# Attention scores in three half-height products per half of the keys, with the keys loaded once

## Chip, core and metric

The kernel runs on one core of a Trainium2 chip. The metric is the device time of one execution in microseconds (us); the median of three runs of the kernel before is 776.71 us (776.66 to 779.36). The core's engines are TensorE (PE in the profile, with its weight loads as a row of their own, PEld), VectorE (DVE), ScalarE (ACT), GpSimd (POOL), and SyncE (SP), which here only issues DMAs.

## What is computed

Attention over 16 heads (2 batches of 8, 576 keys, 64 values per head) in which each query keeps its 32 largest scores, then two dense stages on the result: an expert stage with four experts, and a stage that takes the largest of three products.

```python
scores = scale * np.matmul(q, k.transpose(0, 1, 3, 2))        # (2, 8, 576, 576), 64 summed
kth = np.partition(scores, -32, axis=-1)[..., -32:-31]
scores = np.where(scores >= kth, scores, -1e9)
attn = softmax(scores)                                         # with 1e-9 in the divisor
x = (attn @ v), heads side by side                             # (1152, 512)
for e in range(4):
    out += p[:, e:e+1] * (np.maximum(x @ w1[e], 0) @ w2[e])    # w1 512x1024, w2 1024x512
h = np.maximum(np.maximum(out @ m1, out @ m2), out @ m3)       # m 512x768
y = h @ mo                                                     # 768x512
```

All of it is float32. The kernel keeps float32's accuracy on TensorE by splitting every factor into a rounded high part and a low part (the rest), both of the type fp32r, and by summing products of the parts.

## The kernel before

**Attention** goes by pairs: a pair is one tile of 128 query rows and one head pair `hp` (two heads, `j` = 0 and 1; `hp` runs over 4). There are 9 tiles and so 36 pairs. Tile 4 holds rows of both batches, and its scores are made for each batch and summed (`SLOTS` pads with zeros), so its products are twice as many. Time is divided into slots, eight for a pair; `attention()` puts each step of a pair at a slot: scores 4 to 12 slots ahead of the pair's own first slot, then top-32 on DVE (`topk`, four MAX8 and three MATCH_REPLACE8 per head, L389 and L391), the exponential on ACT, the mask on DVE or POOL (L409, L412, L413), the transposes of the probabilities on PE (`trans_p`, L427 and L432), their copies on ACT (`pt`, L430 and L435), the product with the values (`pv`, L469 and L472) and the transpose of the divisors (`trans_r`, L455).

**Scores** (`Pair.scores`, L368): the queries `qT` = (`qh`, `ql`) lie twice, on rows 0 to 63 and again on rows 64 to 127. The keys lie as `kT`, high part on rows 0 to 63 and low part on rows 64 to 127. So one product over 128 rows gives `ql`·(high + low), a second gives `qh`·(high + low). A head's 576 scores are two halves of 288 columns, each in a PSUM bank of its own (`bank`, six of them): two products for each half, four for a head and batch. All four use the whole array of 128 rows by 128 columns.

**Keys** (`load_k`, `split_k`): `twice` loads the same 64 rows of a head pair to both halves of the partitions (2 DMAs, 14 of them with 288 KB and 4 with 144 KB at the start); ACT rounds all 128 rows (L270, one instruction of 576 columns a head), and POOL subtracts on rows 64 to 127 (L271, one of 64x576 a head). There are 8 such key tiles; the first is split by DVE.

**`pv`** is worth a look, since it is the one place that already divides the array: L472 has the two heads' values, 64 columns each, as weights of products that write rows 0 to 63 and rows 64 to 127 of one bank. They are float32 proper, and each stands in the trace as two products. L469 ahead of them and L455 behind them use the whole array.

**The dense stages** run as a generator, `products()`, in seven phases (four expert phases, three of the last stage); each of their products is three of fp32r (L606 to L608). The planner keeps two clocks: `dve(n)` adds the VectorE time of what was issued, `pe(n)` adds n / 2400 us for n columns on TensorE. After each slot the dense stage is advanced until `clock["pe"]` has caught up with `clock["dve"]`. So the order on PE depends on what `pe()` was told that the scores cost, and it is fixed when the program is built: each engine takes its instructions in that order. ACT, POOL and DVE split the weights (L229, L235); the last stage's weights come as 64-bit numbers and are narrowed in 48 pieces (L200 to L212) during and after the last pairs.

Of the kernel before, what the change touches and what calls it, by code (L numbers as in the profile page):

```python
# [10 lines left out]
F32 = mybir.dt.float32  # L11
F32R = mybir.dt.float32r
U32 = mybir.dt.uint32
I32 = mybir.dt.int32
AF = mybir.ActivationFunctionType
ALU = mybir.AluOpType
# [35 lines left out]
def kernel(  # L52
# [14 lines left out]
    nc = tc.nc  # L67
    B, HP, D, _, S = k.shape
    NT, DM = out.shape
    E = gates.shape[2]  # L70
    P = 128
    KT = DM // P
    FF, FF2 = w1.shape[1] * 256, mo.shape[0] * 256
    SH = S // 2
# [16 lines left out]
    kv = ctx.enter_context(tc.tile_pool(name="kv", bufs=2))  # L91
# [22 lines left out]
    def pe(n):  # L114
        clock["pe"] += n / 2400.0

    def bank(name):
        return pg.tile([P, 512], F32, tag="g", name=name)
# [128 lines left out]
    kraw, kT, vt, qraw, qT = {}, {}, {}, {}, {}  # L247
# [5 lines left out]
    def twice(out, src):  # L253

        for half in range(2):
            nc.sync.dma_start(out=out[half * D:(half + 1) * D], in_=src)

    def load_k(b, hp, heads=slice(0, 2)):
        if not heads.start:
            kraw[b, hp] = kv.tile([P, 2, S], F32, tag="kraw", bufs=1, name="kraw")  # L260
        twice(kraw[b, hp][:, heads], k[b, hp][:, heads])

    def split_k(b, hp, heads=(0, 1), sub=nc.gpsimd.tensor_tensor):

        t = kraw[b, hp]
        if 0 in heads:
            kT[b, hp] = kv.tile([P, 2, S], F32R, tag="kT", bufs=5, name="kT")
        d = kT[b, hp]
        for j in heads:
            nc.scalar.activation(out=d[:, j], in_=t[:, j], func=AF.Copy)  # L270
            sub(out=d[D:, j], in0=t[D:, j], in1=d[D:, j].bitcast(F32), op=ALU.subtract)  # L271

    def load_v(b, hp):
        t = kv.tile([P, 2 * NR, D], F32, tag="v", bufs=5, name="vt")
# [39 lines left out]
    def load_first():  # L314
        for j in range(2):
            load_k(0, 0, slice(j, j + 1))
            load_q(0, 0, slice(j, j + 1))

    def split_first():
        for j in range(2):  # L320
            split_k(0, 0, (j,), nc.vector.tensor_tensor)
            split_q(0, 0, slice(j, j + 1), nc.vector.tensor_tensor)
# [26 lines left out]
    class Pair:  # L349
# [10 lines left out]
        def scores(self, j):  # L360
            srcs = [(b, i) for i, (t, b) in enumerate(SLOTS[self.c]) if t == self.t]
            qs = qT[self.c, self.hp]
            halves = []
            for h in range(2):
                ps = bank("pss")
                mm = [(qs[a][:, j, i * P:(i + 1) * P], kT[b, self.hp][:, j, h * SH:(h + 1) * SH]) for b, i in srcs for a in (1, 0)]
                for i, (l, r) in enumerate(mm):
                    nc.tensor.matmul(ps[:, 0:SH], lhsT=l, rhs=r, start=i == 0, stop=i == len(mm) - 1)  # L368
                pe(SH * len(mm))
                halves.append(ps)  # L370
            s = at.tile([P, 2, SH], F32, tag="s%d" % j, bufs=AHEAD_S, name="s")
            self.s[j] = s

            def copy():
                for h in range(2):
                    nc.scalar.activation(out=s[:, h, :], in_=halves[h][:, 0:SH], func=AF.Copy)
                self.did.add(("s", j))
            return copy
# [115 lines left out]
    def attention():  # L494
# [18 lines left out]
        for key, n in first_use.items():  # L513
            s0 = 8 * n
            if n == 0:
                if key[0] == "k":
                    at_slot(-60, load_first)
                    at_slot(-50, split_first)
                    free["k"] = free["q"] = -50
                    at_slot(s0, load_v, *key[1:])  # L520
                continue
            load, split = (load_k, split_k) if key[0] == "k" else (load_q, split_q)
            at = max(s0 + options(n)["scores"] - (SPLIT_K if key[0] == "k" else SPLIT_Q), free[key[0]] + 2)
            at_slot(max(at - LOAD, free[key[0]] + 1), load, *key[1:])
            at_slot(at, split, *key[1:])
            free[key[0]] = at
            if key[0] == "k":
                at_slot(s0, load_v, *key[1:])
# [110 lines left out]
    def hidden(N):  # L639
        if 2 * N <= 512:  # L640
            ht = hp_.tile([P, 2, 512], F32R, tag="h", bufs=4, name="h")
            return ht[:, 0, 0:2 * N], ht[:, 1, 0:2 * N]

        assert len(x_ready) == len(CHUNKS) * HP and 2 * N <= 2 * MAXS * P
        turn[0] += 1
        hh = kv.tile([P, 2, S], F32R, tag="kT", bufs=5, name="hh")
        hl = qp.tile([P, 2, MAXS * P], F32R, tag=("qh", "ql")[turn[0] % 2], name="hl")
        return [x.rearrange("p a n -> p (a n)")[:, 0:2 * N] for x in (hh, hl)]

    def layer2(ps, wts, hs, N, ti, first=True, last=True):  # L650

# [6 lines left out]
    def experts(n, c):  # L658
# [9 lines left out]
        def half1(i, u):  # L668
            for groups in layer1(weight((c, "a", i, u)), (xh[c], xl[c]), begin.pop((i, u), None)):
                if groups is None:  # L670
                    tick()
                    yield True
            hh, hl = hidden(N)
            count = made_h[0] = made_h[0] + 1
            if ON_POOL_H and not count % ON_POOL_H:
                raw = ms.tile([P, 2 * MAXT * P], F32, tag="tm", bufs=2, name="raw")
                later(lambda: [nc.scalar.activation(out=raw[:, g], in_=ps, func=AF.Relu) for g, ps in groups],
                      lambda: [nc.scalar.activation(out=hh[:, 0:2 * N], in_=raw[:, 0:2 * N], func=AF.Copy),
                               nc.gpsimd.tensor_tensor(out=hl[:, 0:2 * N], in0=raw[:, 0:2 * N], in1=hh[:, 0:2 * N].bitcast(F32), op=ALU.subtract),
                               made.add(("h", n, i, u))])  # L680
                yield hh, hl
                return
            dve(2 * N)
            later(lambda: [nc.scalar.activation(out=hh[:, g], in_=ps, func=AF.Relu) for g, ps in groups],
                  *[lambda: None] * H_LAG,
                  lambda: [nc.vector.scalar_tensor_tensor(out=hl[:, g], in0=ps, scalar=0.0, in1=hh[:, g].bitcast(F32),
                                                          op0=ALU.max, op1=ALU.subtract) for g, ps in groups]
                  + [made.add(("h", n, i, u))])
            yield hh, hl
# [92 lines left out]
    def largest(n, c):  # L782
# [6 lines left out]
        for j in range(FF2 // 256):  # L789

            sub = (nc.vector if j == FF2 // 256 - 1 or (2, c) == PHASES[-1] else nc.gpsimd).tensor_tensor
            hh, hl = hidden(N)
            tm = ms.tile([P, 2 * MAXT * P], F32, tag="tm", bufs=2, name="tm")
            for i in range(3):
                yield from converted(j, i)
                for groups in layer1(weight((c, "c", j, i)), x2):
                    if groups is None:
                        tick()
                    yield True
                dve(2 * N if i else 0)  # L800

                def evac(i=i, groups=groups, tm=tm):
                    for g, ps in groups:
                        if i == 0:
                            nc.scalar.activation(out=tm[:, g], in_=ps, func=AF.Copy)
                        else:
                            nc.vector.tensor_tensor(out=tm[:, g], in0=ps, in1=tm[:, g], op=ALU.max)
                todo = [evac]
                if i == 2:
                    todo += [lambda tm=tm, hh=hh: nc.scalar.activation(out=hh, in_=tm[:, 0:2 * N], func=AF.Copy),  # L810
                             lambda tm=tm, hh=hh, hl=hl, sub=sub: sub(out=hl, in0=tm[:, 0:2 * N], in1=hh.bitcast(F32), op=ALU.subtract)]
                later(*todo)
            hs.append((hh, hl))
# [119 lines left out]
```

## Time and profile before

| what | value |
|---|---|
| median of 3 runs | 776.71 us |
| the profiled execution, its own time | 778.73 us |
| its span, first to last instruction | 776.9 us |
| PE busy / PEld busy | 725.2 us (93%) / 655.3 us (84%) |
| DVE busy | 659.9 us (85%) |
| POOL busy | 541.4 us (70%) |
| ACT busy | 482.3 us (62%) |
| mean granted TensorE clock | 0.978 of full speed |

Busy shares over the whole span say little here, since the program has three stretches. Up to about 94 us only attention runs; from there to about 470 us attention and the expert stage run side by side; behind that the dense stages are alone. Matmuls overlap in the trace: a product's own duration is longer than the distance to the next one's start, and what a product costs in a row of products is that distance, start to start.

### The profile page before, as it was taken

The numbers are of one execution on the slowest core, as the hardware profiler recorded it, in microseconds if no ns is written. First come the engines' busy times: TensorE is split into PE (matmuls) and PEld (weight loads), VectorE is DVE, ScalarE is ACT, GpSimd is POOL, SyncE is SP. The second block draws the span as 40 slices with busy tenths as digits, with TensorE's granted clock in tenths as the row PEclk, the third lists the DMA queues.
The fourth block names the chain that finished last, engine by engine and source line by source line (L and its number), as shares of the span: only waits on it lengthen the run. The fifth ranks groups of instructions, "written<-read, shape, count | busy, mean of one in ns | idle before, by whom it ended". The sixth has DMA issues, their size and how long they took to land. (4 is left out here: it accounts for less than half of the span.)

```text
span 776.9 us, 13519 instructions
## 1 busy us (share of the span) xinstructions
PE 725.2 (93%) x4646; PEld 655.3 (84%) x4646; DVE 659.9 (85%) x1247; ACT 482.3 (62%) x1021; POOL 541.4 (70%) x440
## 2 busy tenths in 40 slices
PE   3666799999999999998999998999999999999998
PEld 2545689988998988887998997989998799899996
DVE  6999999999999999999999996898899994243341
ACT  5666768767786876766777675655565643342441
POOL 3887988889998878778878695675677673343430
PEclk9986699999999999999999999999999999999999
DMA  4430255466645446263554454977667864362421
GB/s 117 105 111 1 60 147 162 137 179 163 195 142 177 126 148 180 87 180 107 150 145 137 137 163 153 301 233 250 221 215 260 252 204 136 102 211 92 156 91 40
DMA packets 48612, 119.91 MB, mean 154 GB/s; under 512 B 7840, under 2 KB 18080, under 8 KB 48544
## 3 DMA queue, kind: packets, MB, share of 16 engines
q1 hardware_dynamic: 40336, 110.40, 46.6%
q10 hardware_dynamic: 8208, 8.65, 3.2%
q8 instruction: 36, 0.59, 0.3%
q14 instruction: 32, 0.26, 0.1%
HBM read 110.38 MB, written 8.65 MB: 153 GB/s over the span
## 5 line engine op out<-in xcount | busy, mean ns | idle before, releaser
L235 POOL TENSOR_TENSOR wlo<-raw,whi 128x512 fp32r<-128x512 f32 x260 | 359.7, 1413 | 129.8 <-ACT whi L229 128.9
L229 ACT ACTIVATE whi<-raw 128x1024 fp32r<-128x1024 f32 x164 | 170.3, 1057 | 41.1 <-DMA raw<-in_w_dram 16.7
L389 DVE MAX8 m<-work 128x8 f32<-128x576 f32 x216 | 154.1, 739 | 0.1
L606 PE MATMUL ps<-xl,whi 128*128 128x256 f32 (+1 forms) x512 | 153.6, 300 | 0.0
L608 PE MATMUL ps<-xh,wlo 128*128 128x256 f32 (+1 forms) x512 | 151.3, 296 | 0.0
L607 PE MATMUL ps<-xh,whi 128*128 128x256 f32 (+1 forms) x512 | 151.2, 295 | 0.0
L235 DVE TENSOR_TENSOR wlo<-raw,whi 128x1024 fp32r<-128x1024 f32 x34 | 52.7, 1550 | 67.2 <-ACT whi L229 55.9
L391 DVE MATCH_REPLACE8 work<-m,work 128x576 f32<-128x576 f32 x144 | 106.0, 736 | 0.0
L607 PEld LDWEIGHTS ps<-xh,whi 128*128 128x128 f32 x512 | 97.2, 190 | 0.9
L606 PEld LDWEIGHTS ps<-xl,whi 128*128 128x128 f32 x512 | 97.1, 190 | 1.0
L608 PEld LDWEIGHTS ps<-xh,wlo 128*128 128x128 f32 x512 | 97.1, 190 | 0.0
L606 PE MATMUL ps<-wlo,h 128*128 128x512 f32 x192 | 77.6, 404 | 0.0
L608 PE MATMUL ps<-whi,h 128*128 128x512 f32 x192 | 75.4, 392 | 0.0
L607 PE MATMUL ps<-whi,h 128*128 128x512 f32 x192 | 75.3, 392 | 0.0
L409 DVE SCALAR_TENSOR_TENSOR p<-s,m,p 128x576 f32<-128x576 f32 x57 | 73.8, 1295 | 0.0
L608 PE MATMUL ps<-x2h,wlo 128*128 128x384 f32 x216 | 72.8, 337 | 0.0
L606 PE MATMUL ps<-x2l,whi 128*128 128x384 f32 x216 | 72.7, 337 | 0.0
L607 PE MATMUL ps<-x2h,whi 128*128 128x384 f32 x216 | 72.6, 336 | 0.0
L368 PE MATMUL pss<-kT,ql 128*128 128x288 f32 x160 | 54.7, 356 | 14.1 <-DVE ql L312 7.5
L212 POOL TENSOR_TENSOR narrow<-narrow,raw 128x256 int32<-128x256 int32 x48 | 40.3, 840 | 39.3 <-DVE narrow L209 10.5
L427 PE MATMUL psp<-ident,p 128*128 128x128 f32 x288 | 49.1, 298 | 17.8 <-POOL p L413 11.9
L427 PEld LDWEIGHTS psp<-ident,p 128*128 128x128 f32 x288 | 37.3, 153 | 24.4 <-POOL p L413 15.5
(97 smaller groups left out, 1632.6 us busy)
## 6 DMA issues: line engine op xcount, KB each, us to landing
raw<-in_w_dram SPq DMA_DIRECT2D x128, 512.0 KB, 3.7
raw<-narrow SPq DMA_DIRECT2D x36, 512.0 KB, 3.4
raw<-in_m_dram SPq DMA_DIRECT2D x36, 256.0 KB, 4.9
narrow<-narrow ACTq DMA_DIRECT2D x48, 128.0 KB, 4.4
kraw<-in_k_dram SPq DMA_DIRECT2D x14, 288.0 KB, 4.5
raw<-in_mo_dram SPq DMA_DIRECT2D x12, 256.0 KB, 4.3
out_dram<-ob ACTq DMA_DIRECT2D x9, 256.0 KB, 2.0
vt<-in_v_dram SPq DMA_DIRECT2D x8, 256.0 KB, 3.7
```

The costliest lines, as they stand in the source:

```text
L212: nc.gpsimd.tensor_tensor(out=out.bitcast(I32), in0=out.bitcast(I32), in1=last, op=ALU.add)
L229: nc.scalar.activation(out=hi, in_=raw, func=AF.Copy)
L235: on.tensor_tensor(out=lo[:, x], in0=raw[:, x], in1=hi[:, x].bitcast(F32), op=ALU.subtract)
L368: nc.tensor.matmul(ps[:, 0:SH], lhsT=l, rhs=r, start=i == 0, stop=i == len(mm) - 1)
L389: nc.vector.max(m[:, 8 * r:8 * r + 8], src)
L391: nc.vector.match_replace(out=self.w[j], in_to_replace=m[:, 8 * r:8 * r + 8], in_values=src, imm_value=NEG)
L409: nc.vector.scalar_tensor_tensor(out=p, in0=s, scalar=kth, in1=p, op0=ALU.is_ge, op1=ALU.mult, accum_out=total)
L427: nc.tensor.transpose(ps[:, r * P:(r + 1) * P], self.p[:, part, part * TAIL + r * P:part * TAIL + (r + 1) * P], ident)
L606: nc.tensor.matmul(ps, lhsT=lh, rhs=rl, start=first, stop=False)
L607: nc.tensor.matmul(ps, lhsT=lh, rhs=rh, start=False, stop=False)
L608: nc.tensor.matmul(ps, lhsT=ll, rhs=rh, start=False, stop=last)
```

## The change

The low part of the keys no longer lies beside the high part on other rows. The new `kT` has four fields for each row: head, part (high, low), and 288 columns. Rows 0 to 63 hold the first half of the keys (columns 0 to 287), rows 64 to 127 the second half. For a head and batch there are now three terms for each half, `ql`·high, `qh`·low and `qh`·high, each a product over 64 rows: the first half's on rows 0 to 63, the second half's on rows 64 to 127, one behind the other in the order, into two banks. The term `ql`·low, which the kernel before computes, is left out. That makes six products for a head and batch where there were four, each on half of the array's rows.

`load_k` loads each half of the keys once, to its rows: 2 DMAs as before, each with half the bytes, in two pieces of 1152 bytes a row instead of one of 4608. `split_k` does both heads in one ACT and one POOL instruction (128 rows, 2x288 columns). `pe()` is told three times 288 columns for a head and batch, where it was told four times. `hidden()`, which uses a `kT` buffer for another purpose, has its view changed to the new shape.

```diff
@@ -257,18 +257,19 @@
 
     def load_k(b, hp, heads=slice(0, 2)):
         if not heads.start:
-            kraw[b, hp] = kv.tile([P, 2, S], F32, tag="kraw", bufs=1, name="kraw")
-        twice(kraw[b, hp][:, heads], k[b, hp][:, heads])
+            kraw[b, hp] = kv.tile([P, 2, SH], F32, tag="kraw", bufs=1, name="kraw")
+        for h in range(2):
+            nc.sync.dma_start(out=kraw[b, hp][h * D:(h + 1) * D, heads], in_=k[b, hp][:, heads, h * SH:(h + 1) * SH])
 
     def split_k(b, hp, heads=(0, 1), sub=nc.gpsimd.tensor_tensor):
 
         t = kraw[b, hp]
         if 0 in heads:
-            kT[b, hp] = kv.tile([P, 2, S], F32R, tag="kT", bufs=5, name="kT")
-        d = kT[b, hp]
-        for j in heads:
-            nc.scalar.activation(out=d[:, j], in_=t[:, j], func=AF.Copy)
-            sub(out=d[D:, j], in0=t[D:, j], in1=d[D:, j].bitcast(F32), op=ALU.subtract)
+            kT[b, hp] = kv.tile([P, 2, 2, SH], F32R, tag="kT", bufs=5, name="kT")
+        h, l = [kT[b, hp][:, heads[0]:heads[-1] + 1, x] for x in range(2)]
+        t = t[:, heads[0]:heads[-1] + 1]
+        nc.scalar.activation(out=h, in_=t, func=AF.Copy)
+        sub(out=l, in0=t, in1=h.bitcast(F32), op=ALU.subtract)
 
     def load_v(b, hp):
         t = kv.tile([P, 2 * NR, D], F32, tag="v", bufs=5, name="vt")
@@ -360,14 +361,13 @@
         def scores(self, j):
             srcs = [(b, i) for i, (t, b) in enumerate(SLOTS[self.c]) if t == self.t]
             qs = qT[self.c, self.hp]
-            halves = []
-            for h in range(2):
-                ps = bank("pss")
-                mm = [(qs[a][:, j, i * P:(i + 1) * P], kT[b, self.hp][:, j, h * SH:(h + 1) * SH]) for b, i in srcs for a in (1, 0)]
-                for i, (l, r) in enumerate(mm):
-                    nc.tensor.matmul(ps[:, 0:SH], lhsT=l, rhs=r, start=i == 0, stop=i == len(mm) - 1)
-                pe(SH * len(mm))
-                halves.append(ps)
+            halves = [bank("pss") for _ in range(2)]
+            mm = [(qs[a][:, j, i * P:(i + 1) * P], kT[b, self.hp][:, j, x]) for b, i in srcs for a, x in ((1, 0), (0, 1), (0, 0))]
+            for i, (l, r) in enumerate(mm):
+                for h, ps in enumerate(halves):
+                    rows = slice(h * D, (h + 1) * D)
+                    nc.tensor.matmul(ps[:, 0:SH], lhsT=l[rows], rhs=r[rows], start=i == 0, stop=i == len(mm) - 1)
+            pe(SH * len(mm))
             s = at.tile([P, 2, SH], F32, tag="s%d" % j, bufs=AHEAD_S, name="s")
             self.s[j] = s
 
@@ -643,9 +643,9 @@
 
         assert len(x_ready) == len(CHUNKS) * HP and 2 * N <= 2 * MAXS * P
         turn[0] += 1
-        hh = kv.tile([P, 2, S], F32R, tag="kT", bufs=5, name="hh")
+        hh = kv.tile([P, 2, 2, SH], F32R, tag="kT", bufs=5, name="hh")
         hl = qp.tile([P, 2, MAXS * P], F32R, tag=("qh", "ql")[turn[0] % 2], name="hl")
-        return [x.rearrange("p a n -> p (a n)")[:, 0:2 * N] for x in (hh, hl)]
+        return hh.rearrange("p a b n -> p (a b n)")[:, 0:2 * N], hl.rearrange("p a n -> p (a n)")[:, 0:2 * N]
 
     def layer2(ps, wts, hs, N, ti, first=True, last=True):
 
```

On PE, the scores of a head between products of the expert stage, about 311 us into the span in the trace of before. Here `pss` is the bank of scores, `ps` one of the dense stages. Before:

```order
L608 MATMUL ps_4019<-whi,h 128x512
L368 MATMUL pss<-kT,ql 128x288
L368 MATMUL pss<-kT,qh 128x288
L368 MATMUL pss<-kT,ql 128x288
L368 MATMUL pss<-kT,qh 128x288
L606 MATMUL ps_4019<-wlo,h 128x512
```

And the same head of the same pair now (the line has become L369; a row's shape is that of the result, and the 64 rows are not seen in it):

```order
L608 MATMUL ps_4141<-whi,h 128x512
L369 MATMUL pss<-kT,ql 128x288 x2
L369 MATMUL pss<-kT,qh 128x288 x4
L606 MATMUL ps_4141<-wlo,h 128x512
L607 MATMUL ps_4141<-whi,h 128x512
```

Six products stand where four stood, and the dense products around them are later ones of the program: up to the last transposes of attention (L427) PE has 1716 dense products in its order now, where it had 1686; the 30 are of 512 columns each.

On PE, the next scores, about 318 us into that span, which come behind the product with the values (`psv`) and the transpose of the divisors (`psr`). Before:

```order
L469 MATMUL psv<-pt_4061,v_last_111 128x128
L472 MATMUL psv<-pt,vt 64x128 x8
L455 MATMUL psr<-ident,rb 128x128
L368 MATMUL pss<-kT,ql 128x288
L368 MATMUL pss<-kT,qh 128x288
L368 MATMUL pss<-kT,ql 128x288
L368 MATMUL pss<-kT,qh 128x288
L427 MATMUL psp<-ident,p 128x128 x4
```

And now:

```order
L469 MATMUL psv<-pt_4178,v_last_111 128x128
L472 MATMUL psv<-pt,vt 64x128 x8
L455 MATMUL psr<-ident,rb 128x128
L369 MATMUL pss<-kT,ql 128x288 x2
L369 MATMUL pss<-kT,qh 128x288 x4
L427 MATMUL psp<-ident,p 128x128 x4
```

The place is the same; products on the whole array stand ahead of the six and behind them.

On POOL, the first key tile that it splits, between the queries' low part `ql` and the first mask. Before:

```order
L312 TENSOR_TENSOR ql<-qraw,qh 128x2x256
L271 TENSOR_TENSOR kT<-kraw,kT 64x576 x2
L412 TENSOR_SCALAR s<-s,m_198 128x576
L413 TENSOR_TENSOR p<-p,s 128x576
L412 TENSOR_SCALAR s<-s,m_211 128x576
```

And now:

```order
L313 TENSOR_TENSOR ql<-qraw,qh 128x2x256
L272 TENSOR_TENSOR kT<-kraw,kT 128x2x288
L412 TENSOR_SCALAR s<-s,m_204 128x576
L413 TENSOR_TENSOR p<-p,s 128x576
L412 TENSOR_SCALAR s<-s,m_217 128x576
```

Two subtractions on 64 rows have become one on 128, at the same place.

## Rows read from the trace of the kernel before

**Rows 1.** Stretches: us; PE, PEld, DVE, ACT, POOL busy; clock; DMA share; GB/s.

```profile
0.00:94.00 94.00, 56.21 (x275) 44.15 (x276) 87.05 (x189) 60.92 (x169) 68.92 (x63) 0.82 0.27 78
94.00:470.00 376.00, 367.74 (x2790) 333.39 (x2787) 375.88 (x775) 275.07 (x592) 315.65 (x251) 1.00 0.51 151
470.00:777.00 307.00, 301.27 (x1584) 277.76 (x1584) 196.95 (x285) 146.30 (x262) 156.87 (x128) 1.00 0.56 182
```

**Rows 2.** What PE waited for from 94 to 470 us: total, times, longest.

```profile
PE psv L469 <- ACT pt L435: 3.9, 5, 1.6
PE psp L427 <- DVE h L686: 2.8, 2, 1.6
PE psp L427 <- DVE p L409: 1.6, 2, 1.1
```

**Rows 3.** Score products with ql after 94 us: ns min/median/max, first and last start.

```profile
L368 PE MATMUL pss<-kT,ql x124: 290/295/382, 94.2 to 452.9; 128*128 128x288 f32 x124
```

**Rows 4.** Timeline of PE, scores between expert products: start, duration, what.

```profile
311.24 0.29 PE L368 MATMUL pss<-kT,ql 128*128 128x288 f32 x1
...
311.64 0.29 PE L368 MATMUL pss<-kT,qh 128*128 128x288 f32 x1
311.77 0.39 PE L606 MATMUL ps<-wlo,h 128*128 128x512 f32 x1
312.00 0.40 PE L607 MATMUL ps<-whi,h 128*128 128x512 f32 x1
```

**Rows 5.** Timeline of PE around the product with the values.

```profile
316.48 0.38 PE L469 MATMUL psv<-pt,v_last 128*128 128x128 f32 x2
316.79 1.09 PE L472 MATMUL psv<-pt,vt 128*64 128x128 f32 x16
317.82 0.33 PE L455 MATMUL psr<-ident,rb 128*128 128x128 f32 x1
317.90 0.38 PE L368 MATMUL pss<-kT,ql 128*128 128x288 f32 x1
...
318.25 0.30 PE L368 MATMUL pss<-kT,ql 128*128 128x288 f32 x1
```

**Rows 6.** Timeline of PE, transposes between expert products.

```profile
313.17 0.60 PE L427 MATMUL psp<-ident,p 128*128 128x128 f32 x4
313.60 0.27 PE L432 MATMUL psp<-ident,p 128*128 128x128 f32 x1
313.63 0.48 PE L606 MATMUL ps<-wlo,h 128*128 128x512 f32 x1
313.95 0.40 PE L607 MATMUL ps<-whi,h 128*128 128x512 f32 x1
```

**Rows 7.** Groups by shape: busy us, mean ns.

```profile
L271 POOL TENSOR_TENSOR kT<-kraw,kT 64x576 fp32r<-64x576 f32 x14 | 19.6, 1423 | 2.3 <-ACT kT L270 1.9
L413 POOL TENSOR_TENSOR p<-p,s 128x576 f32<-128x576 f32 x15 | 21.1, 1407 | 1.3
L270 ACT ACTIVATE kT<-kraw 128x576 fp32r<-128x576 f32 x16 | 10.2, 681 | 6.9 <-DMA kraw<-in_k_dram 6.9
```

**Rows 8.** Timeline of the start, ACT and DVE.

```profile
7.60 0.42 ACT L311 ACTIVATE qh<-qraw 128x256 fp32r<-128x256 f32 x1
7.92 0.69 ACT L376 ACTIVATE s<-pss 128x288 f32<-128x288 f32 x2
...
8.72 0.75 DVE L389 MAX8 m<-s 128x8 f32<-128x576 f32 x1
...
10.66 0.76 DVE L389 MAX8 m<-s 128x8 f32<-128x576 f32 x1 [0.34 <-ACT s L376]
```

**Rows 9.** DMA issues: KB each, median us to landing.

```profile
kraw<-in_k_dram SPq DMA_DIRECT2D x14, 288.0 KB, 4.5
```

## The prediction

> **What bounds the kernel now.** I read the busy time of three stretches first [rows 1]. From 94 to 470 us DVE is busy for 375.88 of 376 us: the top-32 search and what else it does there set how fast attention goes. PE is busy for 367.74 us of the same 376, so 8.3 us of it are free. Behind 470 us PE is nearly full (301.27 of 307, the rest mostly at the very end) and DVE is not: there PE sets the end. Before 94 us PE has 56.21 of 94 and DVE 87.05 (its first 8.72 us are the start [rows 8]). So the end comes as: 94 us of start, 376 us in which DVE sets the pace, and then what dense work PE has left. Work taken off PE between 94 and 470 us does not end that stretch sooner; it helps only if dense work moves forward into the room. Second, the waits of PE in that stretch [rows 2]: 8.3 us in nine waits, all for results that go through DVE (the mask, the hidden layer's low part, the copied transposes), none for POOL, for a DMA, or for a bank of PSUM. Third, PE in order of time, for what score products cost in a row.
>
> **What the scores cost now.** Start to start, four products of 288 columns take 0.53 us (311.24 to 311.77 [rows 4]), 0.1325 each. After 94 us there are 124 with ql [rows 3] and as many with qh, so 62 units of four; 8 of them are the second batch of tile 4 (four head pairs, two heads) and follow their first directly. That is 54 places in PE's order, 46 with one unit and 8 with two.
>
> **What three half-height pairs cost.** No row shows a product on 64 rows. The nearest is L472, which splits the array by columns: 16 products of 128 columns in 1.09 us [rows 5], of which the last takes 0.27 (as the single L432 does [rows 6]), so 0.82 us for 15 steps, 0.055 each. L469, same type and as many columns but on the whole array, has (0.38 - 0.27) = 0.11 a step [rows 5]. So two neighbours that use different halves of the array do run together. Taken over to the rows, a pair costs what one product costs, 0.1325, and a unit three of them, 0.3975: 0.1325 us less than now. The bounds: nothing runs together, 6 x 0.1325 = 0.795; or 0.3975. I take 0.3975, since L472 is the only row with a divided array.
>
> **What the change of the array's shape costs.** From the start of the two L469 (316.48) to the third L368 behind them (318.25) lie 1.77 us [rows 5]. Their steps come to 2 x 0.11 + 8 x 0.11 + 0.11 (L455) + 2 x 0.1325 = 1.475. The other 0.295 us is spent on going to the divided array and back. Where the type and the line change but the array stays whole, nothing is lost: L427 at 313.17 to L607 at 313.95 is 0.78 [rows 6], and five steps of 0.11 and one of 512 columns at 0.23 (311.77 to 312.00 [rows 4]) make 0.78. In the changed order the products ahead of each score place and behind it use the whole array, so each of the 54 places goes there and back. Bounds: 0 and 0.295 a place; I take 0.295, the measured one, though it was measured on columns.
>
> The Trainium skill says the same against this change: in "TensorEngine Tiling (Array Packing)", Key Properties, changing the tiling mode, not just the tile, drains the TensorE. The trace agrees for the column split, with the 0.295 us above; no row shows it for rows. By that sentence the forecast below holds, without it the first rival.
>
> A place with one unit then costs 0.295 + 0.3975 = 0.6925 for 0.53, +0.1625; one with two units 0.295 + 0.795 = 1.09 for 1.06, +0.03. Sum: 46 x 0.1625 + 8 x 0.03 = **+7.7 us of PE work** between 94 and 470 us, where 8.2 us (62 x 0.1325) were to be saved.
>
> **What moves.** The planner is told three quarters of the old price, so it packs dense work more tightly: the order has 30 more dense products of 512 columns ahead of attention's last transposes, 30 x 0.23 = **7.0 us moved** from behind 470 us to before it. That is right only if the scores really become cheaper; at the prices above PE has 367.7 + 7.7 + 7.0 = 382.4 us to do in 376, and passes DVE as the bound of the stretch.
>
> **What is off the path.** POOL: 14 subtractions of 1.42 us become 7 on 128x576, which cost 1.41 in L413 [rows 7]: 9.8 us less. ACT: 16 roundings of 0.68 [rows 7] become 7, and two of half the size at the start: some 5 us less. Neither is worth anything by itself, for PE names neither as what it waits for between 94 and 470 us [rows 2]. If POOL were the cover that is gone, PE would wait for the split weights; POOL is busy 315.65 of 376 [rows 1] and only loses work. SP issues the same number of key DMAs, each half as large, in pieces of 1152 bytes; a key tile lands in 4.5 us now [rows 9] and is asked for 11 slots ahead, over 10 us at eight slots a pair, so 0 either way. PSUM: both banks of a head are opened at once, the first is held some 0.27 us longer; no wait in rows 2 is for a bank, so 0. Start: the first MAX8 at 8.72 us needs the ACT copy that ends at 8.61 and stands behind `qh` at 7.60, whose input the change leaves alone; DVE's subtractions shrink. Between 0 and 0.7 us (the two DVE subtractions at half their length), 0.3 taken.
>
> **The sum.** First stretch 94 - 0.3. Second 382.4 + r, where r is what PE still waits for DVE. Third 307 - 7.0 = 300.0. Together 776.1 + r, against 777 now. r lies between 0 and the present 8.3: PE falls behind by 14.7 us in the stretch, so a wait as long as the longest now (1.6 us [rows 2]) is used up within some 40 us; but once DVE waits for scores, its results come late again. I take r = 2. That gives 778.1 of span against 776.9 of span in the profiled execution, **+1.2 us**. The execution itself took 778.73, 1.8 more than its span, and the median of the runs is 2.0 below it; I add the difference to the median: 776.7 + 1.2 = 777.9, say **778**. With r from 0 to 8 and 0.04 us of doubt for each way in or out (54 x 2 x 0.04 = 4.3), this case lies between 772 and 788.
>
> **Rivals.**
> *The shape costs nothing (faster).* For: L472's price was measured on columns, where weights of 64 columns are loaded; here both halves keep 128. Against: it is the only row there is. A place then costs 0.1325 or 0.265 less, -8.2 us of PE work; 367.7 - 8.2 + 7.0 = 366.5 is under 376, DVE still sets the stretch, and the gain is the moved work alone: 7.0 + 0.3, 769.4.
> *The two weight loads of a pair go one after the other (slower).* Each of the six products brings its own weights of 128 columns, where L472's have 64. A transposed block, load and product of 128 columns, takes 0.11 a step [rows 6], so a load takes at most that, two of them 0.22 a pair; it decides once a load is over half of 0.1325. At 0.22 a place costs 0.955 or 1.615, 46 x 0.425 + 8 x 0.555 = +24.0; the second stretch is 367.7 + 24.0 + 7.0, all three 792.4, +15.5 against the span's 776.9: 792. Against: in L472 two loads of 64 columns fit in a step of 0.11. The Trainium skill, "TensorE: Matmul & The Clock Gate", LDWEIGHTS, has loading time go by columns and not by rows, so that a load of half the rows would be as long as a full one. No row here shows a load of 64 rows.
> *The products do not run together (slower; the change does not do what it says).* Six steps and the 0.295: 1.09 for 0.53, 1.885 for 1.06, +32.4 us; three stretches 800.8, so 800.5 on the median. Against it speaks L472.
>
> **How the numbers follow.** The forecast 0.48, no price for the shape 0.22, loads in turn 0.15, not together 0.12, others (a price between) 0.03. A measurement of this kernel can tell 0.5%, 3.9 us, from no change. Of the forecast's 0.48, 0.35 lie within that, 0.11 above it and 0.02 below. Faster 0.22 + 0.02 = 0.24; same 0.35 + 0.03 = 0.38; slower 0.11 + 0.15 + 0.12 = 0.38. The range goes from the first rival's 769 to 795, above the loads in turn; products that do not run together stay out.
>
> **What would show it.** In the timeline of PE after the change: the two products of a pair start within some 0.01 us, pairs 0.13 apart (right), or six products 0.13 apart (not together), or pairs 0.2 apart (loads in turn). From the last dense product to the second pair of a score place some 0.15 us more than their steps, and as much behind the third: the shape's price. In the busy times by stretch: DVE under full between 94 us and the end of attention, with waits for ACT's copies of scores or for PE, and PE's waits for DVE below 8 us. If DVE stays full and attention ends at about 470 us, PE did not become the bound, and the time is that of the first rival. POOL with 10 us less and no effect on PE's waits would confirm that it covers nothing.

## The result: slower by 0.9%, and the profile after

The changed kernel takes 785.5 us (median of four runs, 783.75 to 786.02), the kernel before 777.9 beside it (776.66 to 779.36): a ratio of 1.0093, with a 95% interval of 1.0065 to 1.0121. That is 7.6 us more. The profiled execution has a span of 781.8 us, 4.9 more than that of before.

Busy time of the changed kernel by stretch; the columns are those of [rows 1].

```profile
0.00:94.00 94.00, 57.43 (x322) 42.21 (x323) 86.90 (x191) 60.22 (x167) 66.09 (x61) 0.78 0.22 65
94.00:470.00 376.00, 374.96 (x2886) 325.87 (x2885) 367.76 (x760) 266.88 (x579) 305.46 (x246) 1.00 0.49 147
470.00:782.00 312.00, 304.22 (x1603) 279.91 (x1601) 202.05 (x298) 150.11 (x269) 157.17 (x128) 0.99 0.53 180
```

Between 94 and 470 us PE and DVE have changed places: PE is busy for 374.96 of 376 us, where it had 367.74, and DVE, which was full, has 8 us free. POOL has 10 us less. What the two waited for from 94 to 475 us says the same (who waits and for whom, total us, times, longest); these lines answer to [rows 2], where PE had 8.3 us of waits and DVE none that matter.

```profile
PE ps L606 <- DVE h L686: 0.5, 1, 0.5
PE psp L427 <- DVE h L686: 0.4, 1, 0.4
PE psv L469 <- ACT pt L435: 0.2, 1, 0.2
...
DVE h L686 <- ACT h L684: 5.1, 7, 1.0
DVE acc L715 <- PE ps L608: 3.1, 6, 0.8
```

PE's waits are down to 1.1 us. DVE now waits for the dense stage's products (ACT's copy `h` stands behind PE's product), and attention's search stands behind that in DVE's order. Attention ends later: the last L427 starts at 481.6 us, that of before at 470.8; dense work starts at 93.6 us (94.8 before), and 300.2 us follow the end of attention (306.1 before).

A score place of the changed kernel between dense products, in PE's order of time; it answers to [rows 4].

```profile
301.13 0.28 PE L608 MATMUL ps<-xh,wlo 128*128 128x256 f32 x1
301.34 0.40 PE L369 MATMUL pss<-kT,ql 64*128 64x288 f32 x2
301.57 0.42 PE L369 MATMUL pss<-kT,qh 64*128 64x288 f32 x4
301.93 0.39 PE L606 MATMUL ps<-xl,whi 128*128 128x256 f32 x1
302.15 0.28 PE L607 MATMUL ps<-xh,whi 128*128 128x256 f32 x1
```

The two products of a pair start 0.003 us apart in the records; one row holds both. From L608 to the second dense product behind the place lie 1.02 us; two dense steps of 0.12 taken off, the place costs 0.78, where four products on the whole array cost 0.53. The pairs are as quick as predicted: the last two are 0.13 apart (four products in 0.42, of which one lasts 0.29). The rest is delay, in four pieces: L608 to the first pair 0.21 for a step of 0.12; first to second pair 0.235 for 0.13; third pair to L606 0.22 for 0.13; L606 to L607 0.22 for 0.12. Together 0.385.

The weight loads of the same place (PEld) show what the pieces are.

```profile
301.01 0.19 PEld L608 LDWEIGHTS ps<-xh,wlo 128*128 128x128 f32 x1
301.33 0.19 PEld L369 LDWEIGHTS pss<-kT,ql 64*128 64x128 f32 x2
301.44 0.32 PEld L369 LDWEIGHTS pss<-kT,qh 64*128 64x128 f32 x4
301.93 0.19 PEld L606 LDWEIGHTS ps<-xl,whi 128*128 128x128 f32 x1 [0.16 <-issue]
302.04 0.19 PEld L607 LDWEIGHTS ps<-xh,whi 128*128 128x128 f32 x1
```

L608's load starts at 301.01, 0.12 ahead of its product, under the product before. The first loads of the place start with their own products (301.33), and so does that of L606 behind it (301.93): they were not done ahead across the change of shape, and the array stood 0.09 us longer. The next loads come 0.11 later, so the first ones took that long, in the open. In front of L472 in the kernel before, with 64 columns of weights, that second piece was 0.05 (the first loads start at 316.79 us, the next at 316.85).

There is a second place where time goes, at the end of attention. DVE of the changed kernel:

```profile
470.26 1.41 DVE L389 MAX8 m<-work 128x8 f32<-128x576 f32 x2
...
472.37 0.80 DVE L409 SCALAR_TENSOR_TENSOR p<-s,m,p 128x576 f32<-128x576 f32 x1
...
475.81 1.76 DVE L235 TENSOR_TENSOR wlo<-raw,whi 128x1024 fp32r<-128x1024 f32 x1 [2.63 <-ACT whi L229]
477.49 0.75 DVE L389 MAX8 m<-work 128x8 f32<-128x576 f32 x1
...
480.00 0.81 DVE L409 SCALAR_TENSOR_TENSOR p<-s,m,p 128x576 f32<-128x576 f32 x1
```

And the same engine of the kernel before:

```profile
469.46 0.87 DVE L409 SCALAR_TENSOR_TENSOR p<-s,m,p 128x576 f32<-128x576 f32 x1
...
479.15 1.78 DVE L235 TENSOR_TENSOR wlo<-raw,whi 128x1024 fp32r<-128x1024 f32 x1 [2.42 <-ACT whi L229]
```

The first split of weights that DVE does (L235; from the fourth dense phase on every second one is DVE's) stood behind attention's last mask (L409). In the changed order it stands between the last two masks: DVE waits 2.63 us there for ACT's rounding, splits for 1.7, and the last head's search and mask stand behind. PE has nothing else to do by then, since the fourth phase needs attention's last result (PE's timeline):

```profile
477.30 0.40 PE L608 MATMUL ps<-whi,h 128*128 128x512 f32 x1
480.96 1.09 PE L427 MATMUL psp<-ident,p 128*128 128x128 f32 x4 [3.26 <-DVE p L409]
```

PE waits 3.26 us, and its four transposes then take 1.09 us for the 0.60 of [rows 6]. The stretch from 480 to 485 us, with the columns of [rows 1], has the reason in the granted clock: 0.50, the lower of its two levels (1.2 of 2.4 GHz). From 475 to 480 us PE had been busy for 2.70 of 5 us; from 485 to 490 us the clock is 0.82 on the mean, from 490 to 500 us 1.00.

```profile
480.00:485.00 5.00, 3.40 (x21) 2.81 (x23) 0.98 (x4) 1.58 (x5) 0.62 (x1) 0.50 0.87 306
```

### The profile page after: what moved, and what is told of

It reads as the page before. It is cut to its first block, busy times and chain, and to the rows that moved or that the text cites. A ratio compares the mean times of both kernels' runs of the same rounds, so it can differ in the third digit from the quotient of the medians.

```text
span 781.8 us, 13830 instructions
## 1 busy us (share of the span) xinstructions
PE 736.6 (94%) x4806; PEld 648.0 (83%) x4806; DVE 656.7 (84%) x1247; ACT 477.2 (61%) x1014; POOL 528.7 (68%) x433
## 4 chain that ended last, share of the span: by engine, by line
PE 78%; DVE 18%; ACT 1%; issue 1%; SPq 1%; DMA 0%; ACTq 0%; DVEq 0%
PE ps L606 21%; PE ps L608 20%; PE ps L607 20%; DVE m L389 8%; DVE work L391 7%; PE pss L369 4%; PE psv L472 3%; PE psp L427 3%; PE pso L608 2%; PE pso L606 2%; PE pso L607 2%; DVE p L409 2%; PE psv L469 1%; PE psr L455 1%; DVE h L686 1%
## 5 line engine op out<-in xcount | busy, mean ns | idle before, releaser
L235 POOL TENSOR_TENSOR wlo<-raw,whi 128x512 fp32r<-128x512 f32 x260 | 359.1, 1410 | 135.2 <-ACT whi L229 127.5
L606 PE MATMUL ps<-xl,whi 128*128 128x256 f32 (+1 forms) x512 | 155.0, 303 | 0.5 <-DVE h L686 0.5
L389 DVE MAX8 m<-work 128x8 f32<-128x576 f32 x216 | 154.5, 742 | 0.1
L608 PE MATMUL ps<-xh,wlo 128*128 128x256 f32 (+1 forms) x512 | 151.3, 296 | 0.0
L607 PE MATMUL ps<-xh,whi 128*128 128x256 f32 (+1 forms) x512 | 151.3, 295 | 0.0
L235 DVE TENSOR_TENSOR wlo<-raw,whi 128x1024 fp32r<-128x1024 f32 x34 | 52.7, 1551 | 64.3 <-ACT whi L229 52.7
L606 PEld LDWEIGHTS ps<-xl,whi 128*128 128x128 f32 x512 | 97.3, 190 | 3.6 <-issue 1.9
L607 PEld LDWEIGHTS ps<-xh,whi 128*128 128x128 f32 x512 | 97.4, 190 | 0.8
L608 PEld LDWEIGHTS ps<-xh,wlo 128*128 128x128 f32 x512 | 97.3, 190 | 0.0
L606 PE MATMUL ps<-wlo,h 128*128 128x512 f32 x192 | 79.3, 413 | 0.0
L607 PE MATMUL ps<-whi,h 128*128 128x512 f32 x192 | 75.4, 393 | 0.0
L608 PE MATMUL ps<-whi,h 128*128 128x512 f32 x192 | 75.3, 392 | 0.0
L608 PE MATMUL ps<-x2h,wlo 128*128 128x384 f32 x216 | 72.8, 337 | 0.0
L606 PE MATMUL ps<-x2l,whi 128*128 128x384 f32 x216 | 72.7, 337 | 0.0
L607 PE MATMUL ps<-x2h,whi 128*128 128x384 f32 x216 | 72.6, 336 | 0.0
L409 DVE SCALAR_TENSOR_TENSOR p<-s,m,p 128x576 f32<-128x576 f32 x57 | 72.1, 1266 | 0.0
L427 PE MATMUL psp<-ident,p 128*128 128x128 f32 x288 | 51.8, 309 | 17.0 <-POOL p L413 12.2
L376 ACT ACTIVATE s<-pss 128x288 f32<-128x288 f32 x144 | 50.9, 409 | 19.3 <-PE pss L369 19.3
L427 PEld LDWEIGHTS psp<-ident,p 128*128 128x128 f32 x288 | 36.6, 156 | 27.4 <-POOL p L413 15.5
```

Source lines behind the costliest of these rows:

```text
L235: on.tensor_tensor(out=lo[:, x], in0=raw[:, x], in1=hi[:, x].bitcast(F32), op=ALU.subtract)
L389: nc.vector.max(m[:, 8 * r:8 * r + 8], src)
L409: nc.vector.scalar_tensor_tensor(out=p, in0=s, scalar=kth, in1=p, op0=ALU.is_ge, op1=ALU.mult, accum_out=total)
L427: nc.tensor.transpose(ps[:, r * P:(r + 1) * P], self.p[:, part, part * TAIL + r * P:part * TAIL + (r + 1) * P], ident)
L606: nc.tensor.matmul(ps, lhsT=lh, rhs=rl, start=first, stop=False)
L607: nc.tensor.matmul(ps, lhsT=lh, rhs=rh, start=False, stop=False)
```

## Experiments

All ratios are to the kernel before on the same chip, whose median moved between 776.8 and 779.9 us from one set of runs to the next; so ratios are compared, not microseconds. My theory after reading the profile was the price of the shape; the rival was that the tighter packing of dense work does the harm.

**The planner's price alone, products of before.**

```diff
-                pe(SH * len(mm))
+                pe(0.75 * SH * len(mm))
```

> Kernel before, its products unchanged; only the planner is told three quarters of the scores' price, as in the changed kernel, so the 30 dense products (7.0 us) move ahead of attention's end. Theory (the shape's price on PE makes the change slower, the moved work by itself is a gain): PE has 367.7 + 7.0 = 374.7 us to do in the 376 in which DVE sets the pace, and behind attention 7.0 us less; 771 to 775 against 777.9 of the kernel before. Rival (the tighter packing is what makes the change slower, because PE gets late for attention): 781 to 786, like the changed kernel.

781.1 us, ratio 1.0046 (1.0025 to 1.0066). The theory failed here: without one product changed, half of the loss is there. Its trace has the same thing at the end of attention, on DVE and on PE (here the transposes still run at the full clock, and the lower one comes behind them: 0.77 on the mean from 480 to 485 us):

```profile
472.31 1.75 DVE L235 TENSOR_TENSOR wlo<-raw,whi 128x1024 fp32r<-128x1024 f32 x1 [2.63 <-ACT whi L229]
...
476.49 0.81 DVE L409 SCALAR_TENSOR_TENSOR p<-s,m,p 128x576 f32<-128x576 f32 x1
...
477.45 0.63 PE L427 MATMUL psp<-ident,p 128*128 128x128 f32 x4 [3.38 <-DVE p L409]
```

**The products alone, planner told the old price.**

```diff
-            pe(SH * len(mm))
+            pe(SH * len(mm) * 4 / 3)
```

> Changed kernel, but the planner is told the old price of the scores, so that dense work stands where it stood in the kernel before. Theory (PE's work counts, wherever it stands): between 94 us and attention's end PE has 367.7 + 11.4 = 379 us to do, just over 376, plus its waits; behind it the old 307; 783 to 786, the same as the changed kernel. Rival (tighter packing makes it slower): back to 777 to 779.

780.4 us, ratio 1.0039 (1.0019 to 1.0060): neither end of what was expected, but the other half. The two halves add up to 1.0085, near the whole change's 1.0093. In this trace the first L235 on DVE stands behind the last mask again. From the first dense product to the last L427, which starts 3.7 us later than before, PE's waits are 2.4 us, where they were 8.7: the products cost PE some 10 us, and its free time took up 6 of them.

**Is it that one split?** The first one that DVE does goes to POOL, with nothing else changed, once with the products of before and the planner told three quarters, once in the changed kernel.

```diff
-            on = nc.vector if late >= 0 and late % 2 else nc.gpsimd
+            on = nc.vector if late >= 2 and late % 2 else nc.gpsimd
```

> Products of the kernel before, planner told three quarters, as in the first experiment; and the one weight split that the tighter plan put on DVE ahead of attention's last masks (it waited 2.6 us for ACT's rounding and ran 1.8) is done by POOL. Theory (that split, queued on DVE ahead of the last masks, holds attention's end, and with it PE, which waits 3.7 us there and falls to half clock): 4 to 5 us less than the 781.1 without this edit, 776 to 777, attention's last transposes at 473 to 474 us where they were at 477.8. Rival (PE is late all along, so that DVE waits for dense products in many places): 780 to 782.

> Changed kernel with the same edit: the first weight split that stood on DVE ahead of attention's last masks is done by POOL, nothing else changed. Theory: 4 to 6 us less than the changed kernel, 779 to 782, attention's last transposes at some 477 us instead of 481.6, and no stretch at half clock behind them. Rival: 785, unchanged.

With the products of before: 776.2 us beside 778.9, ratio 0.9974 (0.9959 to 0.9989). The changed kernel: 780.5, ratio 1.0024 (1.0006 to 1.0042). The edit takes 0.72 and 0.69 points off. The end of attention in the first of the two, on DVE and PE:

```profile
468.72 0.75 DVE L389 MAX8 m<-work 128x8 f32<-128x576 f32 x1
...
472.52 1.42 DVE L409 SCALAR_TENSOR_TENSOR p<-s,m,p 128x576 f32<-128x576 f32 x1
...
474.10 0.63 PE L427 MATMUL psp<-ident,p 128*128 128x128 f32 x4 [0.92 <-DVE p L409]
```

The search goes on without the hole, and PE's wait is 0.92 us. In the changed kernel one expectation missed: with the edit the last transposes start at 480.7 us, not at some 477, and the spans of the two profiles differ by 2.8 us, where the medians differ by 5.0. The traces show why. DVE of the changed kernel with the edit, the counterparts of the two L389 rows shown above:

```profile
472.12 1.41 DVE L389 MAX8 m<-work 128x8 f32<-128x576 f32 x2
...
474.96 0.76 DVE L389 MAX8 m<-work 128x8 f32<-128x576 f32 x1
```

Before the place of the split this trace is 1.86 us late, behind it 2.53 early: the split with its wait was 4.4 us on DVE, and as much in the pair with the products of before. The lateness arises long before the edited instruction. Up to 97 us the two traces run within 0.1 us of each other on DVE, and at 110 us the one with the edit is 1.8 late. In between PE got through 17 products where the other trace has 27, at half the clock (94 to 97 us, without and with the edit):

```profile
94.00:97.00 3.00, 2.85 (x27) 2.52 (x28) 3.00 (x9) 3.00 (x9) 3.00 (x3) 1.00 0.66 180
94.00:97.00 3.00, 3.00 (x17) 2.72 (x16) 3.00 (x9) 3.00 (x9) 3.00 (x3) 0.50 0.62 180
```

Around the end of attention, from 470 to 500 us, the clock with the edit is 1.00, and 298.3 us follow the last L427 instead of 300.2. So these two profiles of nearly the same program differ by some 2 us by the moment at which the clock rose, before the edit comes in at all. The same edit in the kernel before, where that split stands behind the masks anyway:

> Kernel before with the first of the weight splits that DVE does given to POOL, and nothing else. In the order of before that split already stands behind attention's last masks. Theory: no change, within 2 us of before. Rival (the edit is a gain by itself, whatever the order): 772 to 774, 4 us less, as between the two runs with the tighter plan.

Ratio 1.0012 (0.9994 to 1.0031): no change. So the edit is worth something only where the tighter order had moved the split. In this profile the clock fell too, to 0.66 on the mean from 470 to 475 us, behind a wait of 1.47 us; in that of before it stayed at 1.00 behind one of 1.46. So the fall behind the wait is not a sure part of what the split costs.

**A milder price**, seven eighths, with the same edit and the products of before.

> Products of the kernel before, planner told seven eighths of the price instead of three quarters, first split on POOL. Theory (the moved dense work is a small gain once attention's end is not held): between before and the run with three quarters, 1 to 3 us under before. Rival (the middle is better than either end, since DVE is held less): 4 us or more under before.

778.4 us, ratio 1.0004 (0.9986 to 1.0021): nothing, where 1 to 3 us were expected. The run with three quarters and the first split on POOL stays the fastest of all kernels tried, by 0.26% under the kernel before.

**Where the pairs' gain goes.** Two kernels with the order of the old price; neither computes the scores of the reference (their expectations say what they compute). In the first all six products use the whole array:

```diff
-                    rows = slice(h * D, (h + 1) * D)
+                    rows = slice(0, P)
```

> Changed kernel with the old price told to the planner, and each of the six products over all 128 rows (so scores of both halves of the keys are summed; the output is not the reference's). No product on part of the array, so nothing is paid for its shape and nothing runs together: a place costs six steps of 0.1325, 0.795 us, with two units 1.59, no delay ahead or behind. Theory: within 0.02 us of what a place with three pairs and the shape's price costs between dense products (0.785), 0.4 us more where it has two units, so 3 to 6 us above the run with pairs (780.4). Rival (the delays around a place come from the products' number, not the shape): delays stay, a place costs 1.18, 20 us more.

785.2 us, ratio 1.0090 (1.0065 to 1.0114), 0.5 points over the run with pairs. PE's timeline:

```profile
316.16 0.40 PE L608 MATMUL ps<-whi,h 128*128 128x512 f32 x1
316.40 0.42 PE L369 MATMUL pss<-kT,ql 128*128 128x288 f32 x2
316.66 0.70 PE L369 MATMUL pss<-kT,qh 128*128 128x288 f32 x4
317.19 0.39 PE L606 MATMUL ps<-wlo,h 128*128 128x512 f32 x1
317.42 0.39 PE L607 MATMUL ps<-whi,h 128*128 128x512 f32 x1
```

1.26 us less two dense steps of 0.233 is 0.79: six steps of 0.132 and no delay on either side. So the delays belong to the shape. In the second all six lie on rows 0 to 63:

```diff
-                    rows = slice(h * D, (h + 1) * D)
+                    rows = slice(0, D)
```

> Changed kernel with the old price told to the planner, and all six products on rows 0 to 63 (the second half of the scores is made from the first half's keys; the output is not the reference's). Theory (two products run together because they lie on different rows): six steps 0.13 us apart and the shape's price of 0.385, 1.18 us a place for 0.785. Rival (they run together because they write different banks): starts of a pair still 0.003 us apart, 0.785 a place.

805.6 us in a single execution, so without an interval. PE's timeline:

```profile
312.06 0.39 PE L608 MATMUL ps<-whi,h 128*128 128x512 f32 x1
312.38 0.53 PE L369 MATMUL pss<-kT,ql 64*128 64x288 f32 x2
312.75 0.69 PE L369 MATMUL pss<-kT,qh 64*128 64x288 f32 x4
313.37 0.50 PE L606 MATMUL ps<-wlo,h 128*128 128x512 f32 x1
313.71 0.39 PE L607 MATMUL ps<-whi,h 128*128 128x512 f32 x1
```

1.65 less 0.466 is 1.18: the shape's 0.385 and six steps in turn, though neighbours write two different banks as before. It is the different rows that let two products run together. One place, then, costs 0.53 with four products on the whole array, 0.79 with six, 0.78 with three pairs, 1.18 with six half-height ones in turn: what pairing wins over six full products, the change of shape takes back.

**Half as many changes of shape.** The scores of both heads of a pair at one place, in the changed kernel and, as a control, with the products of before (planner told three quarters in both).

```diff
-                two(b0 + o["scores"], pr.scores, j)
+                two(s0 + o["scores"], pr.scores, j)
```

> As the run with only the planner's price changed, but the scores of both heads of a pair stand at one place of PE's order (the second head's move up to the first's). Whole array throughout, so no price for a shape. Theory: within 3 us of that run, since nothing is saved on PE. Rival (the place of the second head's scores matters by itself, through DVE or the banks): more than 3 us away from it, to either side.

> Changed kernel with the scores of both heads of a pair at one place of PE's order: 27 places after the start where there were 54, the same products. Theory (0.36 to 0.39 us for going to the 64-row shape and back, once a place): about 10 us less on PE, 775 to 778, against 785.5 of the changed kernel. Rival (the time goes with the products or their weight loads, not with the places): 784 to 787.

Both theories on the times missed: 791.2 us with the products of before, ratio 1.0167 (1.0134 to 1.0199), on the side of the rival, and 790.6 with pairs, 1.0174 (1.0145 to 1.0204), outside theory and rival. The control says why for the most part: four banks are filled at once, and PE waits for ACT's copies to free them (the control's waits of PE, 94 to 475 us; before has no such line):

```profile
PE psp L432 <- ACT s L376: 4.1, 4, 3.0
PE psp L427 <- ACT s L376: 3.5, 1, 3.5
```

The two ratios differ by 0.07 points with 27 places, where it is 0.47 with 54 (1.0093 against 1.0046). That alone settles nothing: the intervals overlap, and PE, busy for 363 to 364 of 376 us, had room to hide more work. The place itself does settle it. From L608 to the second dense product behind two heads' scores, with pairs and then with the products of before:

```profile
308.13 0.28 PE L608 MATMUL ps<-xh,wlo 128*128 128x256 f32 x1
...
308.84 0.29 PE L369 MATMUL pss<-kT,ql 64*128 64x288 f32 x2
...
309.55 0.28 PE L607 MATMUL ps<-xh,whi 128*128 128x256 f32 x1
```

```profile
307.37 0.28 PE L608 MATMUL ps<-xh,wlo 128*128 128x256 f32 x1
...
308.67 0.28 PE L607 MATMUL ps<-xh,whi 128*128 128x256 f32 x1
```

1.42 us against 1.30: two heads at one place cost 0.12 more with pairs (0.385 paid once, less 2 x 0.13 saved), where one head costs 0.26 more. The second head's first pair (308.84) lasts 0.29 and not 0.40, so it has no load in the open. The price goes by the place, not by the product, as the theory had it.

**The keys' work on POOL and ACT.** Each key tile rounded and subtracted twice in place, old price told.

```diff
-        nc.scalar.activation(out=h, in_=t, func=AF.Copy)
-        sub(out=l, in0=t, in1=h.bitcast(F32), op=ALU.subtract)
+        for _ in range(2):
+            nc.scalar.activation(out=h, in_=t, func=AF.Copy)
+            sub(out=l, in0=t, in1=h.bitcast(F32), op=ALU.subtract)
```

> Changed kernel with the old price told to the planner, and each key tile rounded and subtracted twice, so that POOL has 9.8 us and ACT some 5 us of work again, as in the kernel before. Theory (that work lies on no path): 780.4, as without it, within 2 us. Rival (POOL's and ACT's relief hides a part of what the scores cost): 784 or more.

790.5 us, ratio 1.0163 (1.0138 to 1.0187). This would speak for the rival, but the edit adds a wait that neither kernel has: the second rounding overwrites what the first subtraction reads. ACT's waits in this run:

```profile
ACT kT L272 <- POOL kT L273: 25.8, 7, 4.8
```

So it was made again with the second instructions writing buffers of their own:

> Changed kernel with the old price told to the planner; for each key tile but the first, ACT and POOL do their instruction a second time, into buffers of 2-byte numbers that nobody reads, each straight behind its first, with no wait on the other engine. So POOL has its 9.8 us and ACT its 5 us of key work again. In the run that split the keys twice in place, ACT's second rounding waited for POOL's first subtraction, 25.8 us in all, which the kernel before does not have. Theory (the key work lies on no path, and that wait made the run slow): 780 to 783, within 2 us of the run without the work. Rival (the relief of POOL and ACT hides part of what the scores cost): 785 to 790.

781.1 us, ratio 1.0012 (0.9998 to 1.0025), with the work really there:

```profile
L278 POOL TENSOR_TENSOR again<-kraw,kT 128x576 bf16<-128x576 f32 x7 | 10.0, 1434 | 0.0
...
L275 ACT ACTIVATE again<-kraw 128x576 bf16<-128x576 f32 x7 | 4.8, 679 | 0.0
```

Ten microseconds of POOL and five of ACT cost nothing that these runs can tell. What made the run in place slow was the wait on ACT's queue: its searches on DVE fall behind those of the run with pairs and the old price in steps, by 4.2 us up to 97 us and by 8.4 up to 290, as the seven key tiles come. The first tile, which only that run splits twice, is not it: its first MAX8 starts at 8.58 us, where the other's starts at 8.64.

## Why the prediction was right in its range and wrong in its likeliest case

785.5 us lies in the range of 769 to 795, and slower by over 0.5% had a chance of 0.38. The likeliest case, 778 and no change, was not what came; the sign of its +1.2 us was right and its size was not. That the range holds the result is partly luck: its upper part stood there for loads in turn, which did not come, and no rival had the weight split.

- **What bounds the kernel** was right, and so was what follows: PE passed DVE as the bound of the middle stretch [rows 1], 374.96 of 376 against 367.76.
- **Three pairs at 0.1325** was right: pairs are 0.13 apart, and the two rivals that hang on it (products not together, loads in turn) did not come about. Taking L472's columns [rows 5] for rows held.
- **The price of the shape** had the right mechanism and the wrong size: 0.295 taken, 0.385 measured between dense products. The 0.295 came from neighbours whose first loads in the open are 64 columns or float32 transposes, 0.05 each; here they are 128 columns of fp32r, 0.105, both going in and coming out. Behind L455 the place is 0.20 dearer than before, between dense products 0.26. Over the stretch, from the first dense product to the last L427, PE's work (the time less its waits) is 367.3 us before and 377.4 with the products alone: 10.1 more, where the sum had 7.7.
- **What moves** is the step that failed. It counted the 30 products and PE's time, 7.0 us, and put at nothing what they do to the other queues: a tighter plan also moves the weight split that belongs to the next phase, on DVE, ahead of the last masks. That one instruction with its wait, 4.4 us on DVE, is worth 0.7% in two pairs of kernels. The prediction asked what the change means for POOL, ACT, SP and the banks, not what the new order puts on DVE's queue.
- **The moved work's gain** was overrated too. With the split out of the way, 7.0 us moved gave 0.26%, some 2 us. In that profile 7.8 us less follow attention, but the stretch before its end is 3.4 us longer (379.4 for 376.0): PE's waits fell only from 8.7 us to 5.7, and DVE waits too. The r of the sum, taken as 2, was 4.4 in the changed kernel: 1.1 up to 475 us, and the 3.3 behind the split.
- **Off the path**: POOL, ACT and DMA at zero was right (the run with the work put back), and the subtraction on 128 rows took 1.43 us for 1.41 [rows 7].
- **The sum by stretch**: 93.7, 384.4 and 300.0 were forecast for the profile, with cuts at 94 and 470 us. Cut at the first dense product and the last L427, the kernel before has 94.8, 376.0 and 306.1, the changed one 93.6, 388.0 and 300.2. In the middle 12.1 us were added: 16.4 of work (7.0 moved, the rest the shape's) less 4.3 of waits. Of the 5.9 taken off behind it the lower clock holds back some 2 (298.3 in the run with the split on POOL). The first rival, no price for the shape, fell with the four delays around every place.

## To carry to other kernels

Count what a divided array saves against one entry and one exit for every place where it stands alone among full products: here 0.13 us saved and 0.385 paid. Products that use different rows do run together, so there is a gain only where enough pairs follow each other: two heads at one place still lost 0.12 us, and by these figures (0.13 saved a head, 0.385 paid a place) the gain begins at the third or fourth, an estimate. When a planner is told a lower price, look at every engine's order, and first for instructions of the next phase that now stand, with their waits, ahead of the last ones of this phase on an in-order queue.

## What the runs showed of the hardware that was not expected

- Two products on different halves of the rows, with 288 columns of fp32r each, start 0.003 us apart and take the time of one (0.13 us a pair); two on the same rows take turns, 0.13 us each, though they write different banks.
- Weights are not loaded ahead across a change of the array's shape: 0.09 us until the first load and then the load itself in the open, 0.105 us for 128 columns of fp32r (64 rows or 128), 0.05 for 64 columns, each way. The Trainium skill, "TensorEngine Tiling (Array Packing)", Key Properties, says that changing the tiling mode drains the TensorE. The traces agree, for a division by rows (0.385 us for the way in and out) as for one by columns (0.295).
- Seven ACT instructions that wait for POOL, 25.8 us in all, cost 10 us of the kernel's time, and as much work without the wait cost nothing that the runs can tell.
- Executions of nearly the same program get the full clock at different moments: up to 97 us two traces are within 0.1 us of each other on DVE, the granted clock from 94 to 97 us is 1.00 (2.4 GHz) in one and 0.50 (1.2 GHz) in the other, and behind it they are 1.8 us apart. Before that, from 85 to 91 us, PE was busy for 5.31 of 6 us in both, at 0.51 and 0.50.
